# Layernorm, sliding attention and top-2 experts in one kernel: the first eight token tiles of QKV in a written order, two column groups in turn

## The chip, the cores and the metric

One core of a Trainium2 chip runs the whole program as one launch. The metric is the device time of that launch in microseconds (us); a time is the median of the runs shown. TensorE is called PE below, VectorE DVE, ScalarE ACT, GpSimd POOL; SyncE (SP) starts most of the DMAs.

## The reference

The input x is one sequence of 2048 tokens of 512 numbers, all in f32. The layernorm of x goes into two branches, and both are added to x:

```python
def attention(x, wqkv, wo):      # 32 heads of 16; 8 keys at distances 0, 2, .., 14
    q, k, v = split(x @ wqkv)
    idx = pos[:, None] - (arange(8) * 2)[None, :]
    logits = einsum("bhsd,bhswd->bhsw", q, k[idx]) * 16 ** -0.5   # -1e9 where idx < 0
    return einsum("bhsw,bhswd->bhsd", softmax(logits), v[idx]) @ wo

def experts(x, w_gate, w1, w2):  # 8 experts, 512 -> 1792 -> 512
    top2 = argsort(-(x @ w_gate))[:, :2]; gates = softmax(their logits)
    return sum over e of gate_e * (silu(x @ w1[e]) @ w2[e])

xn = layernorm(x)
out = x + attention(xn, wqkv, wo) + experts(xn, w_gate, w1, w2)
```

## The kernel before

**Numbers.** Every f32 factor of a matrix product is split into an f16 high and an f16 low part, and a product is three matmuls: high by high, high by low, low by high. The rows of `xh_j` hold both parts of token tile j after the layernorm; `xnT` holds the same turned (8 blocks of 128 × 128 per tile: four of the high, four of the low part). `wq_cg` holds the split columns of `wqkv` that belong to column group cg: 384 high columns (q, k and v of four chunks of two heads), for group 0 also 16 columns of the gate, and 384 low ones. `split_wq` makes them from the loaded `wqs_cg`, the high part on ACT, the low on DVE.

**Tiles.** The tokens lie in 16 tiles j of 128. `norm_tile(j)` takes `x_{j // 2}` (each load brings two tiles) and does: the moments on DVE (L226, L228), the root on ACT (L230), reciprocal and normalisation on DVE (L231, L233), the high part on ACT and the low part on DVE for tiles 0 and 1 and on POOL for the others (L235, L236). Tiles 0 to 5 are turned by PE (L241), eight blocks into a PSUM tile `pt_j`, and copied in one piece by ACT (odd tiles) or DVE (even ones). Tiles 6 to 15 are turned by one DMA each on SP (L248). `store_xn(j)` writes `xh_j` to `xr` in DRAM, for the experts' gathers.

**Products.** `qkv_tile(cg, j)` does twelve matmuls for one tile and one column group (L262 to L264), two evictions on ACT into `qe` and `ke` (L270, L272; two buffers each, of four tiles), for group 0 the 16 gate logits on DVE (L276), and after every fourth tile two stores on SP, of `qe` to `qd` and of `ke` to `kvd` (L281, L282). PSUM has six banks in turn for it.

**Order.** Group 0 comes first for all 16 tiles, then groups 1, 2 and 3. In this part of the program the tile framework's scheduler sets the order on each engine, from the order of the code and its own reckoning of when operands are ready. Routing follows group 0's last gate logits; POOL gathers the experts' token rows from `xr`, and SP turns them; the first of these turns is put behind the store of group 2's last four tiles (`FIRST`). From group 2 on, each tile is followed by pieces of the attention on DVE: `attend(QATT)` takes pieces from a list (`atoms`) as long as the sum of their costs is behind the sum granted. The experts follow, in an order written by hand, in steps of one hidden block: ACT makes the high part of the hidden values `hh` (L723, L724), DVE the low (L730) and the low part of the weights (L148), and in each step `EATT` (one number for large experts, one for small) is granted to the attention that is left. The pieces there are, among others, a product over 2048 columns (L567, L593) and the sums that fold it (L600).

**Start.** `warm_up(n, tag)` runs n products of zeros on PE, 12 at the start and 8 behind `norm_tile(1)`'s code. The loads on SP are: x_0 in two halves, the four parts of `wqs_0` (192 KB each), the gate's columns, then x_1 and on.

Of the kernel before, what the change touches and what calls it, by code (L numbers as in the profile page):

```python
# [9 lines left out]
F16 = mybir.dt.float16  # L10
# [47 lines left out]
def layer_kernel(ctx: ExitStack, tc, x, wqkv, wo, wg, w1, w2, out):  # L58
# [23 lines left out]
    root = cp.tile([P, 1], F32, name="root")  # L82
    nc.scalar.activation(root, eps, AF.Sqrt)
# [129 lines left out]
    load_x(0)
    load_wq(0)
    for g in range(1, 4):
        load_x(g)

    xhs = {}
# [3 lines left out]

    def norm_tile(j):
        xt = xg4[j // 2][:, j % 2, :]
        st = fre.tile([P, 6], F32, name=f"bs_{j}", tag="bs")
        nc.vector.bn_stats(st, xt)  # L226
        mv = fre.tile([P, 2], F32, name=f"mv_{j}", tag="mv")
        nc.vector.bn_aggr(mv, st)  # L228
        rs = fre.tile([P, 1], F32, name=f"rs_{j}", tag="rs")
        nc.scalar.activation(rs, mv[:, 1:2], AF.Sqrt, bias=eps, scale=1.0 / (SX * SX))  # L230
        nc.vector.reciprocal(rs, rs)  # L231
        xn = fre.tile([P, D], F32, name=f"xn_{j}", tag="xn")
        nc.vector.tensor_scalar(xn, xt, mv[:, 0:1], rs, op0=ALU.subtract, op1=ALU.mult)  # L233
        xh = fre.tile([P, 2, D], F16, name=f"xh_{j}", tag="xh", bufs=8)
        nc.scalar.copy(xh[:, 0, :], xn)  # L235
        (nc.vector if j < NDV else nc.gpsimd).tensor_tensor(xh[:, 1, :], xn, xh[:, 0, :], op=ALU.subtract)  # L236
        xhs[j] = xh
        if j < NPE:
            pt = py.tile([P, 2 * KB, P], F16, name=f"pt_{j}", tag="misc" if j % 2 else "yt")
            for a in range(2 * KB):  # L240
                nc.tensor.transpose(pt[:, a, :], xh[:, a // KB, (a % KB) * P:(a % KB + 1) * P], ident)  # L241
            dst = xnT[:, :, j * P:(j + 1) * P]
            if j % 2 == NEV:
                nc.scalar.copy(dst, pt)
            else:
                nc.vector.tensor_copy(dst, pt)  # L246
            return
        nc.sync.dma_start_transpose(out=xnT[:, :, j * P:(j + 1) * P], in_=xh.rearrange("p a d -> p (a d)"))  # L248

    tags = [(pu, "up"), (pu, "up"), (py, "y0"), (py, "y1"), (py, "y2"), (py, "y3")]  # L250
    ev, stored = {}, {}
    last = {"pe": None, "act": None, "dve": None, "dve0": None, "up": None}

    def qkv_tile(cg, j):
        pp, tg = tags[j % len(tags)]
        ps = pp.tile([P, 512], F32, name=f"pq_{cg}_{j}", tag=tg)
        t = wq[cg]
        n = 400 if cg == 0 else 384
        for kb in range(KB):
            xh = xnT[:, kb, j * P:(j + 1) * P]  # L260
            xl = xnT[:, KB + kb, j * P:(j + 1) * P]
            nc.tensor.matmul(ps[:, 0:n], xh, t[:, kb, 0:n], start=kb == 0, stop=False)  # L262
            nc.tensor.matmul(ps[:, 0:384], xh, t[:, kb, 400:784], start=False, stop=False)  # L263
            nc.tensor.matmul(ps[:, 0:n], xl, t[:, kb, 0:n], start=False, stop=kb == KB - 1)  # L264
# [5 lines left out]
        nc.scalar.activation(qe[:, :, j % 4, :], ps[:, 0:128].rearrange("p (c d) -> p c d", d=H2),  # L270
                             AF.Copy, scale=1.0 / (SW * SX))
        last["act"] = nc.scalar.activation(ke[:, :, j % 4, :, :].rearrange("p c a d -> p a c d"),  # L272
                             ps[:, 128:384].rearrange("p (a c d) -> p a c d", a=2, d=H2),
                             AF.Copy, scale=1.0 / (SW * SX))
        if cg == 0:
            nc.vector.tensor_scalar(glog[:, j, :], ps[:, 384:400], 1.0 / (SW * SX), None, op0=ALU.mult)  # L276
        if j % 4 == 3:
            qv = qd.rearrange("c (p j) d -> p c (j d)", j=NJ)
            kv = kvd[:, 16:, :].rearrange("c (p j) d -> p c (j d)", j=NJ)
            cs = slice(4 * cg, 4 * cg + 4)  # L280
            nc.sync.dma_start(qv[:, cs, g * 4 * H2:(g + 1) * 4 * H2], qe.rearrange("p c j d -> p c (j d)"))  # L281
            stored[cg, g] = nc.sync.dma_start(kv[:, cs, g * 8 * H2:(g + 1) * 8 * H2],  # L282
                                              ke.rearrange("p c j a d -> p c (j a d)"))

    for j in range(NJ):
        if j % 2 == 0 and j // 2 + 4 < NJ // 2:
            load_x(j // 2 + 4)
        norm_tile(j)
        if j == 0:
            split_wq(0)  # L290
        if j == 1:
            warm_up(8, "y1")
        if j == 8:
            load_wq(1)
        if j == 13:
            split_wq(1)
        if j == 6:
            fills()
        if j >= 5:
            store_xn(j - 5)  # L300
        if j > 1:
            qkv_tile(0, j - 2)
    qkv_tile(0, NJ - 2)
    qkv_tile(0, NJ - 1)
    for j in range(NJ - 5, NJ):
        store_xn(j)
# [742 lines left out]
```

## Time and profile before

| | |
|---|---|
| median of 3 runs | 797.95 us (797.6 to 799.4) |
| the profiled execution | 798.24 us, of it 796.4 from first to last instruction |
| PE, DVE, ACT, POOL busy | 779.9, 642.4, 379.0, 105.5 us |
| granted PE clock, mean | 0.997 |
| QKV's first product | 12.96 us after the span's start |
| QKV's last product ends, experts begin | 147.35 us |

A row of the profile names a group of instructions by line, engine, operation and tiles (output <- inputs), or one of them with its start and length. "Idle before" is the time for which the engine stood still just ahead of it, and the arrow names what ended that. L12 is line 12 of the kernel before, unless the text says otherwise.

### The profile page before, as it was taken

The page shows a single profiled execution, that of the slowest core. Times are in us where ns is not written, and L with a number is a line of the kernel's source. Part 1 is how long each engine was busy: PE and PEld are TensorE (multiplying, and loading weights), DVE is VectorE, ACT ScalarE, POOL GpSimd, SP SyncE. Part 2 cuts the span into 40 slices and gives each one's busy share as a digit, 9 for nine tenths or more (in the row PEclk, how much of TensorE's full clock was granted, in tenths as well). Part 3 has the DMA queues.
Part 4 walks back from the last instruction along what each step waited for, and adds up shares of the span by engine and source line. Part 5 has one row for each costly group of instructions (what it writes and reads, how often), then busy time and mean ns, then how long its engine had stood idle before and what let it go on. Part 6 is the DMA issues. An engine that isn't in the chain of part 4 may idle for free.

```text
span 796.4 us, 13794 instructions
## 1 busy us (share of the span) xinstructions
PE 779.9 (98%) x5318; PEld 427.2 (54%) x5318; DVE 642.4 (81%) x915; ACT 379.0 (48%) x706; POOL 105.5 (13%) x118
## 2 busy tenths in 40 slices
PE   7899999999999999999999999999999999999996
PEld 3556666555555555555555555555555555555543
DVE  7929998389888889799789879887999898736363
ACT  4644423564647364736364545545554645544100
POOL 3510502002000300030012000100100000023450
PEclk9999999999999999999999999999999999999999
DMA  8999949558347925573489446744955552594583
GB/s 288 253 295 317 330 159 246 156 144 238 110 142 191 290 81 169 169 232 111 135 220 257 150 136 185 219 156 128 272 174 169 158 155 85 160 329 165 157 281 117
DMA packets 152389, 153.89 MB, mean 193 GB/s; under 512 B 68000, under 2 KB 119456, under 8 KB 151808
## 3 DMA queue, kind: packets, MB, share of 16 engines
q1 hardware_dynamic: 147104, 136.09, 58.4%
q0 software_dynamic: 5216, 16.88, 7.2%
q8 instruction: 43, 0.70, 0.4%
q14 instruction: 26, 0.21, 0.1%
HBM read 108.12 MB, written 29.52 MB: 173 GB/s over the span
## 4 chain that ended last, share of the span: by engine, by line
PE 91%; DVE 3%; DMA 1%; ACT 1%; issue 1%; SPq 0%; POOL 0%; DVEq 0%; POOLq 0%; ACTq 0%
PE pu L718 12%; PE pu L720 12%; PE pu L719 12%; PE y L761 9%; PE y L763 9%; PE y L762 9%; PE pq L262 4%; PE pq L264 4%; PE pq L263 4%; PE yt L743 3%; PE yt L745 3%; PE yt L744 3%; PE pw L955 2%; PE pw L957 2%; PE pw L958 2%
## 5 line engine op out<-in xcount | busy, mean ns | idle before, releaser
L723 ACT ACTIVATE pu<-pu 128x512 f32<-128x512 f32 (+4 forms) x154 | 72.7, 472 | 249.2 <-PE pu L720 249.0
L718 PE MATMUL pu<-xgt,w 128*128 128x512 f16 (+4 forms) x616 | 185.0, 322 | 1.2 <-DVE hh L730 1.0
L719 PE MATMUL pu<-xgt,w 128*128 128x512 f16 (+4 forms) x616 | 185.3, 322 | 0.0
L720 PE MATMUL pu<-xgt,w 128*128 128x512 f16 (+4 forms) x616 | 181.0, 322 | 0.0
L148 DVE SCALAR_TENSOR_TENSOR w<-s,w 128x1024 f16<-128x1024 f32 x112 | 136.2, 1218 | 3.7 <-ACT w L143 3.5
L730 DVE SCALAR_TENSOR_TENSOR hh<-pu,hh 128x512 f16<-128x512 f32 (+4 forms) x154 | 80.3, 544 | 68.7 <-ACT hh L724 68.4
L763 PE MATMUL y<-w,hh 128*128 128x512 f16 x336 | 127.3, 379 | 0.0
L762 PE MATMUL y<-w,hh 128*128 128x512 f16 x336 | 127.3, 379 | 0.0
L761 PE MATMUL y<-w,hh 128*128 128x512 f16 x336 | 127.2, 379 | 0.0
L143 ACT ACTIVATE w<-s 128x1024 f16<-128x1024 f32 x112 | 116.9, 1048 | 2.8 <-DMA s<-in_B_w 2.8
L687 POOL DMA_INDIRECT xg<-xr,lis x35 | 51.6, 1473 | 482.2 <-DMA xgt<-xg 434.6
L262 PE MATMUL pq<-wq,xnT 128*128 128x384 f16 (+1 forms) x256 | 84.6, 330 | 5.0 <-DVE xnT L246 4.4
L720 PEld LDWEIGHTS <-w 128*128 128x128 f16 x616 | 57.3, 97 | 51.4
L264 PE MATMUL pq<-wq,xnT 128*128 128x384 f16 (+1 forms) x256 | 84.4, 330 | 0.0
L263 PE MATMUL pq<-wq,xnT 128*128 128x384 f16 x256 | 84.0, 328 | 0.0
L745 PE MATMUL yt<-hh,w 128*128 128x160 f16 (+4 forms) x448 | 83.6, 222 | 0.0
L743 PE MATMUL yt<-hh,w 128*128 128x160 f16 (+4 forms) x448 | 83.5, 222 | 0.0
L744 PE MATMUL yt<-hh,w 128*128 128x160 f16 (+4 forms) x448 | 83.5, 222 | 0.0
L719 PEld LDWEIGHTS <-w 128*128 128x128 f16 x616 | 57.3, 97 | 46.1 <-issue 2.0
L718 PEld LDWEIGHTS <-w 128*128 128x128 f16 x616 | 58.1, 97 | 44.4
L724 ACT ACTIVATE hh<-pu 128x512 f16<-128x512 f32 (+4 forms) x154 | 74.6, 484 | 4.9
L593 DVE TENSOR_TENSOR pv<-kvt,at 128x2048 f32<-128x2048 f32 x32 | 72.7, 2285 | 0.4
(189 smaller groups left out, 1033.5 us busy)
## 6 DMA issues: line engine op xcount, KB each, us to landing
s<-in_B_w SPq DMA_DIRECT2D x112, 512.0 KB, 3.9
kvt<-kvd SPq DMA_DIRECT2D x16, 960.0 KB, 5.3
kvd<-ke SPq DMA_DIRECT2D x16, 512.0 KB, 4.0
yd<-ys SPq DMA_DIRECT2D x24, 256.0 KB, 2.2
xr<-xh SPq DMA_DIRECT2D x16, 256.0 KB, 4.4
qd<-qe SPq DMA_DIRECT2D x16, 256.0 KB, 3.8
qt<-qd SPq DMA_DIRECT2D x16, 256.0 KB, 4.4
acc<-in_A_x SPq DMA_DIRECT2D x4, 1024.0 KB, 14.1
```

The lines of the kernel that those rows point to most:

```text
L143: nc.scalar.activation(w[:, :, 0, :], st, AF.Copy, scale=SW)
L148: nc.vector.scalar_tensor_tensor(w[:, :, 1, :], st, SW, w[:, :, 0, :], op0=ALU.mult, op1=ALU.subtract)
L262: nc.tensor.matmul(ps[:, 0:n], xh, t[:, kb, 0:n], start=kb == 0, stop=False)
L263: nc.tensor.matmul(ps[:, 0:384], xh, t[:, kb, 400:784], start=False, stop=False)
L264: nc.tensor.matmul(ps[:, 0:n], xl, t[:, kb, 0:n], start=False, stop=kb == KB - 1)
L718: last["pe"] = nc.tensor.matmul(ps, a_[:, kb, 0, fs], xh, start=kb == 0, stop=False)
L719: nc.tensor.matmul(ps, a_[:, kb, 0, fs], xl, start=False, stop=False)
L720: nc.tensor.matmul(ps, a_[:, kb, 1, fs], xh, start=False, stop=kb == KB - 1)
L745: nc.tensor.matmul(dst, b_[:, 1, cs], hi, start=False, stop=sp, skip_group_check=True)
L761: nc.tensor.matmul(ym[t], hi, b_[:, 0, :], start=st, stop=False)
L762: nc.tensor.matmul(ym[t], hi, b_[:, 1, :], start=False, stop=False)
L763: nc.tensor.matmul(ym[t], lo, b_[:, 0, :], start=False, stop=sp)
```

## The change

The first eight tiles (`NFIRST = 8`) are written by hand inside a block in which the order of the code is the order on PE, ACT, DVE, SP and POOL. In it both column groups 0 and 1 are computed for a tile before the next one; the later loop for group 1 starts at tile 8. `norm_tile` is cut into functions (`moments`, `deviation`, `normalize`, `x_high`, `x_low`, `turn_x`, `turned_x`, `turn_dma`), `qkv_tile` into `qkv_products`, `qkv_out` and `gate_out`. Further: `wqs_0` is loaded from ACT's queue, x_1 and `wqs_1` follow x_0 on SP; five tiles (`NPE`) instead of six are turned by PE, and each turned tile is copied in two halves, the high by ACT, the low by DVE; low parts are on POOL except for tile 0; the gate's columns are split on POOL; tile 0's products come by kind (high parts, low parts of x, low parts of weights, then eight products of 16 gate columns); `qe` and `ke` have their own tiles per column group out of the same two buffers; 15 warm-up products instead of 20; `QATT` and `EATT` have new values.

```diff
-QATT = 1.3
-EATT = (3.1, 2.78)
-NPE = 6
-NDV = 2
-NEV = 1
+QATT = 1.1
+EATT = (3.15, 2.86)
+NFIRST = 8
+NPE = 5
...
+    def qkv_product(cg, j, kb, pair, cols, first, end):
+        a, lo = pair
+        ps, t = pq[cg, j], wq[cg]
+        nc.tensor.matmul(ps[:, cols], xnT[:, a * KB + kb, j * P:(j + 1) * P],
+                         t[:, kb, 400:784] if lo else t[:, kb, cols], start=first, stop=end, skip_group_check=True)
...
+    def turned_x(j, a, copy):
+        copy(xnT[:, a * KB:(a + 1) * KB, j * P:(j + 1) * P], pts[j][:, a * KB:(a + 1) * KB, :])
...
+    load_x(0)
+    load_wq(0, (0, 1), nc.scalar)
+    nc.scalar.activation(root, eps, AF.Sqrt)
+    load_wq(0, (2, 3), nc.scalar)
+    load_x(1)
+    nc.sync.dma_start(gs, wg.rearrange("(kb p) e -> p kb e", p=P))
+    load_wq(1)
+    load_x(2)
+    load_x(3)
+    warm_up(WARM, "y0")
+    moments(0)
+    deviation(0)
+    wq_high(0, 0)
+    moments(1)
+    deviation(1)
+    normalize(0)
+    x_high(0)
...
+    for j in range(2, NFIRST):
+        qkv_products(0, j)
+        if j < 6:
+            load_x(j + 2)
+        if j + 2 < NFIRST:
+            moments(j + 2)
+            deviation(j + 2)
+        qkv_out(1, j - 1)
+        if j + 1 < NPE:
+            turn_x(j + 1, 0)
+            turn_x(j + 1, 1)
+            turned_x(j + 1, 0, act)
+            turned_x(j + 1, 1, dve)
+        if j + 2 < NFIRST:
+            normalize(j + 2)
+            x_high(j + 2)
+            x_low(j + 2, gp)
+            if j + 2 >= NPE:
+                turn_dma(j + 2)
+        qkv_products(1, j)
+        qkv_out(0, j)
+        gate_out(j)
+        store_xn(j - 2)
+    qkv_out(1, NFIRST - 1)
...
-        for j in range(NJ):
+        for j in range(NFIRST if cg == 1 else 0, NJ):
             qkv_tile(cg, j)
             if (cg, j) >= (2, 0):
                 attend(QATT)
```

The order on SP around the first tiles that the DMA turns. Rows are instructions in the order of the queue, with their line in the kernel that they belong to; `qd` and `kvd` are the stores (column group and group of four tiles in the second name), `xr` the row stores. Before, from tile 5's row store on:

```order
L221 DMA xr_68<-xh_5_374 128x1024
L248 DMA_TRANSPOSE xnT_144<-xh_6_417 128x8x128
L281 DMA qd_66<-qe_0_0_282 128x4x128
L282 DMA kvd_67<-ke_0_0_283 128x4x256
L221 DMA xr_68<-xh_6_417 128x1024
L248 DMA_TRANSPOSE xnT_144<-xh_7_451 128x8x128
```

After:

```order
L250 DMA_TRANSPOSE xnT_142<-xh_5_459 128x8x128
L298 DMA qd_66<-qe_0_0_292 128x4x128
L299 DMA kvd_67<-ke_0_0_293 128x4x256
L214 DMA xr_68<-xh_1_219 128x1024
L169 DMA x_6_495<-in_A_x 128x1024
L298 DMA qd_66<-qe_1_0_361 128x4x128
L299 DMA kvd_67<-ke_1_0_362 128x4x256
L250 DMA_TRANSPOSE xnT_142<-xh_6_510 128x8x128
```

Between the first two transposes stood three transfers, and six stand there now, with the stores of two column groups and an x load among them.

The order on DVE in the same place. Before, tiles 2 to 5 go in pairs, with the moments ahead (from the low part of tile 1 on):

```order
L226 BN_STATS bs_2_247<-x_1_173 128x6
L226 BN_STATS bs_3_287<-x_1_173 128x6
L228 BN_AGGR mv_2_249<-bs_2_247 128x2
L246 COPY xnT_144<-pt_0_193 128x8x128
L228 BN_AGGR mv_3_289<-bs_3_287 128x2
L226 BN_STATS bs_4_327<-x_2_175 128x6
L226 BN_STATS bs_5_365<-x_2_175 128x6
L231 RECIPROCAL rs_2_251<-rs_2_251 128x1
L231 RECIPROCAL rs_3_291<-rs_3_291 128x1
L233 TENSOR_SCALAR xn_2_254<-x_1_173,mv_2_249,rs_2_251 128x512
```

After, one tile at a time; the piece around tile 5, with the half copy of tile 4 (`pt_4`):

```order
L218 BN_STATS bs_5_437<-x_2_171 128x6
L220 BN_AGGR mv_5_439<-bs_5_437 128x2
L247 COPY xnT_142<-pt_4_445 128x4x128
L228 RECIPROCAL rs_5_441<-rs_5_441 128x1
L230 TENSOR_SCALAR xn_5_457<-x_2_171,mv_5_439,rs_5_441 128x512
L303 TENSOR_SCALAR glog_143<-pq_0_3_422 128x16
L218 BN_STATS bs_6_497<-x_3_173 128x6
```

Tile 0's turned copy stood behind the moments of tiles 2 and 3; now a tile's normalisation stands behind the half copy of the tile ahead of it.

The order on DVE where the experts begin: low parts of the first hidden blocks (`hh_0_0`, `hh_0_1`), of the weights (`w2_0_0`), and a piece of the attention (`pv`). Before:

```order
L730 SCALAR_TENSOR_TENSOR hh_0_0_2005<-pu_0_0_0_2006,hh_0_0_2005 128x512
L730 SCALAR_TENSOR_TENSOR hh_0_0_2005<-pu_0_0_512_2019,hh_0_0_2005 128x48
L600 TENSOR_TENSOR pv_1_0_1863<-pv_1_0_1863 128x8x64
L148 SCALAR_TENSOR_TENSOR w2_0_0_2040<-s2_0_0_1991,w2_0_0_2040 128x2x512
L730 SCALAR_TENSOR_TENSOR hh_0_1_2044<-pu_0_1_0_2045,hh_0_1_2044 128x512
```

After:

```order
L856 SCALAR_TENSOR_TENSOR hh_0_0_1999<-pu_0_0_0_2000,hh_0_0_1999 128x512
L856 SCALAR_TENSOR_TENSOR hh_0_0_1999<-pu_0_0_512_2013,hh_0_0_1999 128x48
L719 TENSOR_TENSOR pv_1_0_2036<-kvt_1_1379,at_1_1537 128x2048
L145 SCALAR_TENSOR_TENSOR w2_0_0_2034<-s2_0_0_1986,w2_0_0_2034 128x2x512
L856 SCALAR_TENSOR_TENSOR hh_0_1_2039<-pu_0_1_0_2040,hh_0_1_2039 128x512
```

The piece between the two hidden blocks was a fold over 512 columns and is now a product over 2048; the attention as a whole has moved back.

More of the change, by code (lines that the diff above doesn't have):

```diff
@@ L213, in layer_kernel, with load_wq @@
[L213 to L218, printed above, removed]
+    wv = wqkv.rearrange("(kb p) (t c) -> p kb t c", p=P, t=3)
+    def load_wq(cg, kbs=range(KB), queue=nc.sync):
+        if cg not in wqs:
+            wqs[cg] = (fre if cg < 2 else frp).tile([P, KB, 3, P], F32, name=f"wqs_{cg}",
+                                                    tag="wqs", bufs=2 if cg < 2 else 1)
+            wq[cg] = frp.tile([P, KB, 784], F16, name=f"wq_{cg}", tag="wq")
+        for kb in kbs:
+            queue.dma_start(wqs[cg][:, kb], wv[:, kb, :, cg * P:(cg + 1) * P])
@@ L220, in store_xn, with split_gate @@
+    def split_gate():
+        t = wq[0]
+        nc.gpsimd.tensor_scalar(gs, gs, SW, None, op0=ALU.mult)
+        nc.gpsimd.tensor_copy(t[:, :, 384:392], gs)
+        nc.gpsimd.tensor_tensor(t[:, :, 392:400], gs, t[:, :, 384:392], op=ALU.subtract)
+    xhs, mvs, rss, xns, pts = {}, {}, {}, {}, {}
     def store_xn(j):
         nc.sync.dma_start(xrv[:, j, :], xhs[j].rearrange("p a d -> p (a d)"))
-    def norm_tile(j):
[L224 to L248, printed above, removed]
@@ new lines, in x_high, with x_low, turn_x @@
+    def x_high(j):
+        xhs[j] = fre.tile([P, 2, D], F16, name=f"xh_{j}", tag="xh", bufs=8)
+        nc.scalar.copy(xhs[j][:, 0, :], xns[j])
+    def x_low(j, engine):
+        engine.tensor_tensor(xhs[j][:, 1, :], xns[j], xhs[j][:, 0, :], op=ALU.subtract)
+    def turn_x(j, a):
+        if a == 0:
+            pts[j] = py.tile([P, 2 * KB, P], F16, name=f"pt_{j}", tag="misc" if j % 2 else "yt")
+        for kb in range(KB):
+            nc.tensor.transpose(pts[j][:, a * KB + kb, :], xhs[j][:, a, kb * P:(kb + 1) * P], ident)
@@ new lines, in layer_kernel @@
+    start_cm.__enter__()
+    act, dve, gp = nc.scalar.copy, nc.vector.tensor_copy, nc.gpsimd
+    root = cp.tile([P, 1], F32, name="root")
+    load_x(0)
[13 more added lines that the diff above has]
+    deviation(1)
@@ new lines, in layer_kernel @@
+    normalize(0)
+    x_high(0)
+    normalize(1)
+    wq_high(0, 1)
+    turn_x(0, 0)
+    warm_up(2, "y1")
+    x_low(0, nc.vector)
+    x_high(1)
+    x_low(1, gp)
+    turn_x(0, 1)
+    warm_up(1, "y2")
+    turned_x(0, 0, act)
+    wq_low(0, 0)
+    turned_x(0, 1, dve)
+    for kb in range(1, KB):
+        if kb > 1:
+            wq_high(0, kb)
+        wq_low(0, kb)
+    qkv_bank(0, 0)
+    part = slice(0, 384)
+    for kb in range(KB):
+        qkv_product(0, 0, kb, (0, 0), part, kb == 0, False)
@@ new lines, in layer_kernel @@
+    for kb in range(KB):
+        qkv_product(0, 0, kb, (1, 0), part, False, False)
+    turn_x(1, 0)
+    turn_x(1, 1)
+    turned_x(1, 0, act)
+    turned_x(1, 1, dve)
+    split_gate()
+    for kb in range(KB):
+        qkv_product(0, 0, kb, (0, 1), part, False, kb == KB - 1)
+    for kb in range(KB):
+        for a in range(2):
+            qkv_product(0, 0, kb, (a, 0), slice(384, 400), False, kb == KB - 1 and a == 1)
+    qkv_products(0, 1)
+    wq_high(1, 0)
+    moments(2)
+    deviation(2)
@@ L304, in layer_kernel @@
     qkv_tile(0, NJ - 1)
-    for j in range(NJ - 5, NJ):
+    for j in range(NJ - 2, NJ):
         store_xn(j)
```

141 lines of the change are left out of this document (85 added, 56 removed).

## The prediction

> **What bounds the kernel now.** I read the page's first part and its chain, then a table of stretches, then that chain in order of time, and only then the groups of the early stretch. The page: TensorE is busy nearly all the time.
>
> ```profile
> span 796.4 us, 13794 instructions
> PE 779.9 (98%) x5318; PEld 427.2 (54%) x5318; DVE 642.4 (81%) x915; ACT 379.0 (48%) x706; POOL 105.5 (13%) x118
> PE 91%; DVE 3%; DMA 1%; ACT 1%; issue 1%; SPq 0%; POOL 0%; DVEq 0%; POOLq 0%; ACTq 0%
> ```
>
> So a change of order can win only where PE idles or runs slowly. The table shows where (start:end, length, then busy time of PE, its weight loads, DVE, ACT, POOL; granted clock, DMA share, GB/s):
>
> ```profile
> 5.70:9.20 3.50, 2.83 (x15) 1.16 (x13) 2.87 (x9) 3.33 (x8) 0.00 (x0) 1.00 0.96 251
> 9.20:12.70 3.50, 1.19 (x12) 0.68 (x12) 3.33 (x8) 1.36 (x3) 0.00 (x0) 1.00 1.01 375
> 12.96:16.10 3.14, 3.13 (x10) 1.49 (x11) 3.14 (x11) 0.91 (x2) 0.56 (x1) 0.50 1.03 364
> 16.10:30.00 13.90, 10.70 (x85) 6.86 (x83) 12.70 (x32) 10.38 (x27) 7.20 (x7) 1.00 0.94 278
> 30.00:46.88 16.88, 16.21 (x97) 9.12 (x95) 10.18 (x30) 9.52 (x30) 8.64 (x8) 1.00 1.16 239
> 46.88:147.35 100.47, 100.47 (x646) 60.67 (x647) 80.66 (x220) 36.26 (x117) 14.75 (x10) 1.00 0.86 269
> 160.00:780.00 620.00, 619.41 (x4296) 334.28 (x4294) 514.12 (x575) 306.31 (x501) 69.36 (x57) 1.00 0.62 180
> ```
>
> ```profile
> 12.96 0.52 PE L262 MATMUL pq<-wq,xnT 128*128 128x400 f16 x1 [1.82 <-DVE xnT L246]
> ```
>
> QKV's first product starts at 12.96. Between there and 46.88 PE loses 1.57 (3.14 us at half clock) + 3.20 (13.90 − 10.70) + 0.67 = 5.4 us. From 46.88 to the end of QKV (147.35), and in the experts, it loses nothing. So the most the change can gain is these 5.4 us and an earlier first product.
>
> **The start.** Rows of the chain (start, length) and of the timeline:
>
> ```profile
> 5.08 5.86 DMA x<-in_A_x
> 3.74 1.35 DVE L226 BATCH_NORM_STATS2 bs<-x 128x6 f32<-128x512 f32 x2 [1.56 <-DMA x<-in_A_x]
> 10.15 0.40 PE L241 MATMUL pt<-ident,xh 128*128 128x128 f16 x4 [0.45 <-DVE xh L236]
> 21.64 0.55 DVE L233 TENSOR_SCALAR xn<-x,mv,rs 128x512 f32<-128x512 f32 x1
> ```
>
> And the groups up to 54 us (busy, mean ns):
>
> ```profile
> L236 POOL TENSOR_TENSOR xh<-xn,xh 128x512 f16<-128x512 f32 x14 | 16.4, 1182 | 20.7 <-ACT xh L235 20.7
> L226 DVE BATCH_NORM_STATS2 bs<-x 128x6 f32<-128x512 f32 x16 | 10.7, 685 | 1.8 <-DMA x<-in_A_x 1.7
> L235 ACT CAST xh<-xn 128x512 f16<-128x512 f32 x16 | 9.7, 614 | 6.9 <-DVE xn L233 6.0 <-ACT rs L230 0.5 <-ACT ke L272 0.4
> L272 ACT ACTIVATE ke<-pq 128x256 f32<-128x256 f32 x16 | 6.0, 377 | 0.0
> L270 ACT ACTIVATE qe<-pq 128x128 f32<-128x128 f32 x16 | 4.4, 272 | 11.0 <-PE pq L264 9.5 <-issue 1.5
> L244 ACT COPY xnT<-pt 128x1024 f16<-128x1024 f16 x3 | 3.0, 1003 | 1.9 <-PE pt L241 1.9
> L228 DVE BATCH_NORM_AGGREGATE mv<-bs 128x2 f32<-128x6 f32 x16 | 2.7, 174 | 0.0
> L231 DVE RECIPROCAL rs<-rs 128x1 f32<-128x1 f32 x16 | 2.2, 147 | 0.6 <-ACT rs L230 0.5
> L246 DVE COPY xnT<-pt 128x1024 f16<-128x1024 f16 x3 | 2.0, 667 | 0.0
> L236 DVE TENSOR_TENSOR xh<-xn,xh 128x512 f16<-128x512 f32 x2 | 1.3, 686 | 0.0
> ```
>
> Today the chain goes through an x load that lands at 10.94 (5.08 + 5.86): DVE takes the moments of tiles 2 and 3 before it copies tile 0's turned block. The written order puts these behind tile 0, and the gate's split on POOL. DVE runs the moments of tile 1 before tile 0's reciprocal, so tile 0 waits for x_0's second half. That half is used at 3.74 + 0.69 = 4.4 today. The first 384 KB of weights now leave from ScalarE's queue at the same moment; at the 334 GB/s of the row below they cost that half up to 1.15 us. From 5.6: 0.69 + 0.17 (moments), 0.15, 0.55, 0.61 (high), 0.69 (low), 0.40 (turn), and a half copy on ACT of 0.58 (1.003 less four times the 0.105 by which a 128-column eviction is dearer), with some 0.06 of handing over at each of eight steps: 9.9. Gain 3.1 us; 2.3 if the weights' high and low parts come late, 4.2 if the weights cost x_0 nothing. The Trainium skill, page "DMA: Bandwidth & Descriptors", section "Issuing engines are not separate DMA queues", speaks against the other queue: transfers that different engines start share the same 16 DMA engines and interleave, and only the sequencer's issue time is saved. By it the gain is the 3.1, and without such sharing it would be the 4.2; no trace of before shows weights on ScalarE's queue.
>
> **The clock at the start.** In 9.20:12.70 PE was busy 1.19 of 3.50 and the clock was halved just behind it; in 5.70:9.20 it was busy 2.83 and stayed at full. In the changed order PE has between its twelve warm-up products (ending at about 6) and 9.9 only eight turns (0.8) and three warm-up products (about 1.0): in 5.7:9.2 some 1.6 of 3.5 us, nearer to the 1.19 than to the 2.83. I take the half clock for 9.2 to 12.7. It costs 2.8 / 2 = 1.4, less about 0.3 of waits for low weights that it covers: 1.1 (0 if the clock stays).
>
> **Column groups in turn.** PE's work is the same, +0.5 for eight products of the gate's 16 columns (at 0.06, about the 0.10 per turn of the row above less its handing over). In return each tile feeds 3.95 us of PE, not 2.0 (rows below), so the work on a tile 1 to 4 (DVE 0.69 + 0.17 + 0.15 + 0.55 + 0.39 = 2.0, ACT 0.61 + 0.58 + two evictions of 0.65 = 2.5) is covered: all of the 5.4 us goes. I keep 1.0 for small waits inside tiles 0 to 2 (weights' highs, a low part on POOL that now takes 1.18 where DVE took 0.69). If that cover were gone it would be the 3.20 again.
>
> **Tiles 5 to 7.** Tile 5 is now turned by the DMA, not by PE. The rows for it (landing of the transposes, PE's pace between two stores that are four tiles apart, rate, sizes):
>
> ```profile
> DMA to landing us min/median/max: 3.4/4.0/5.7
> 101.06 0.36 SPq L281 DMA_DIRECT2D qd<-qe  x1
> 108.86 0.36 SPq L281 DMA_DIRECT2D qd<-qe  x1
> 41.15 5.68 DMA xnT<-xh
> DMA packets 4492, 5.01 MB, mean 334 GB/s; under 512 B 1029, under 2 KB 3466, under 8 KB 4492
> x<-in_A_x SPq DMA_DIRECT2D x7, 512.0 KB, 7.8
> xr<-xh SPq DMA_DIRECT2D x11, 256.0 KB, 4.1
> kvd<-ke SPq DMA_DIRECT2D x3, 512.0 KB, 3.8
> qd<-qe SPq DMA_DIRECT2D x3, 256.0 KB, 3.9
> ```
>
> A tile of groups 1 to 3 takes PE 7.80 / 4 = 1.95, one of group 0 with eight of its twelve products 400 instead of 384 columns wide 2.00.
>
> - *Tile 5.* Its normalisation stands on DVE behind tile 4's turned half, and that behind the half on ACT. From PE's turn of tile 4: ACT's previous eviction 0.25, halves 0.58 + 0.39, reciprocal 0.15, normalise 0.55, high 0.61, low on POOL 1.18, transpose 4.0, handing over 0.35: 8.1 us. Meanwhile PE has three products: 1.95 + 2.00 + 1.95 = 5.9. Stall 2.2 (1.6 with the landing at 3.4, 3.9 at 5.7).
> - *Tile 6.* On SP's queue its transpose stands behind six transfers of 256, 512, 256, 512, 256 and 512 KB (the stores of both groups' tiles 0 to 3, a row store, an x load): 2304 KB, 7.1 us at 334 GB/s, against 3.95 us of cover in tile 5's two products. The nearest row is the one at 41.15: behind a 256 and a 512 KB store a transpose took 5.68, 2.3 above the least of 3.4, which is 768 KB at 334. Stall 7.1 + 0.5 − 3.95 = 3.7 (1.0 if the stores have half drained while SP waited for tile 5; 4.3 if the transposes too take engine time).
> - *Tile 7.* ACT cannot evict group 0's tile 4 until a store of group 0 has landed (two buffers), and tile 7's high part stands behind that eviction: 0.61 + 1.18 + 4.0 after it. Stall 1.2 (0 to 1.4). A tile behind (12): 0.5.
>
> Together 7.6. The transposes themselves are free if they land in time; they do not. Row stores, x loads and the second group's weights (4 × 192 KB early on SP) cost PE nothing else.
>
> **The experts' first steps.** Rows: attention steps on DVE, PE's wait for DVE and the wait of routing's gathers:
>
> ```profile
> L593 DVE TENSOR_TENSOR pv<-kvt,at 128x2048 f32<-128x2048 f32 x32 | 72.7, 2285 | 0.4
> 153.45 0.68 DVE L600 TENSOR_TENSOR pv<-pv 128x512 f32<-128x512 f32 x1
> PE pu L718 <- DVE hh L730: 1.0, 2, 0.6
> POOL xg L687 <- DMA qd<-qe: 43.6, 1, 43.6
> ```
>
> With 1.1 in place of 1.3 per QKV tile, 32 × 0.2 = 6.4 us of attention move into the experts. There DVE is at 514 of 620, and the two new rates (3.15, 2.86) spread them, 0.05 and 0.08 more a step, under the 17% that is idle: nothing. But behind the first hidden block DVE now has a 2.29 step where it had 0.68, and the second block's w2 and hidden values stand behind it: 1.6 later. PE waits there already (the 0.6), so little hides it, though two banks are in turn: +0.8, the middle of 0 and 1.6. The gate's logits come some eight products of group 1 (15.6 us) later, which routing can take: its gathers stood still for 43.6 us behind a store.
>
> **Sum** against the profiled execution: −3.1 (start) − 5.4 (losses of before) + 1.1 (clock) + 0.5 + 1.0 + 7.6 + 0.8 = +2.5. The profiled execution took 798.24, 0.29 over the median of the runs shown (797.95): 800.7, or 800.45 from the median. I say 800.5.
>
> **Rivals.**
> - *Transposes in time (faster).* The place is tile 5's transpose against the end of tile 4's second product, and from there SP's queue. For it: DVE and ACT are idle for 40% of 30:46.88, so the chain could start earlier than I have it. Against: the row at 41.15, and the order, which ties tile 5 to PE's turn of tile 4. With no stalls: 2.5 − 7.6 = −5.1, 793; with a third of them: 795.5. It decides where tile 5's landing is under 5.9 after the turn, and 2304 KB drain in 4 us, 576 GB/s against the 375 that is the most in these rows.
> - *Only tile 5 and half of tile 6.* SP issues the stores early, so half of the bytes have gone when tile 6 is ready: stalls 4.4 rather than 7.6: 797.3, no change. For it: the stores wait for nothing late and can drain while tile 6 is made. Against: all stand behind tile 5's transpose on SP, which issues in order.
> - *The clock halves in the gaps too.* PE idles 3.7 us before tile 6, more than the 2.3 of the 3.50 that brought the half clock at 12.96. Then 3.4 us at half, 1.7 lost, part of it in tile 7's wait: +1 to +1.7, 802. The Trainium skill, page "TensorE: Matmul & The Clock Gate", section "🎯 Why this matters for your kernels", warns of PE gaps above some 3 us between bursts, and puts the window of the gate at about 3.4 us; the trace agrees at 12.96:16.10 (3.14 us at 0.50).
> - *The change does not bring its data earlier*: x_0 comes at 5.6 or later and the start gains 2.3; +0.8, inside my range.
>
> **Chances.** As forecast, 799.3 (the clock stays) to 802: 0.45. Clock in the gaps, 802 to 804: 0.15. Half of the stalls (797.3): 0.20. Transposes in time (793 to 796): 0.20. The range, 795.0 to 803.5, leaves out half of the last case and the top of the second. A measurement can tell 0.2% (1.6 us) from no change: faster is below 796.35, slower above 799.55. From the cases: faster 0.22, within 0.18, slower 0.60. The likeliest case's own range is 799.3 to 802.
>
> **What the changed profile would show.** First product near 9.9, clock 0.50 in part of 9 to 13; PE without gaps from tile 1 to tile 4's second product; then waits of PE on the DMA of xnT at tile 5 (2), 6 (3.7) and 7 (1); QKV's end at 148 to 150 rather than 147.35; a wait of PE on hidden values at the second or third block. If the waits on xnT sum to under 4 us I am wrong on SP's queue; if PE shows no half clock, on the start; if QKV ends on time and the end does not, on the experts.

## The result, and the profile after

The changed kernel takes 808.1 us (807.06 to 810.61, 4 runs) against 797.98 (797.6 to 799.4, 4 runs): the ratio is 1.013, 95% interval 1.0112 to 1.0148. It is slower, as forecast, but by 10 us where 2.5 were forecast, and outside the range. Lines and times below are of the profiled execution of 807.98.

The page after, its span, its row of engines and its chain by engine:

```profile
span 806.3 us, 13773 instructions
PE 782.1 (97%) x5313; PEld 427.3 (53%) x5313; DVE 641.5 (80%) x914; ACT 378.4 (47%) x708; POOL 113.5 (14%) x122
PE 80%; DVE 10%; DMA 4%; ACT 2%; issue 2%; SPq 1%; POOL 1%; ACTq 0%; DVEq 0%; POOLq 0%
```

PE does nearly the same work in 10 us more, and DVE has gone from 3% to 10% of the chain. The table of stretches of the same execution (columns as before the change):

```profile
5.70:9.20 3.50, 1.71 (x13) 0.62 (x11) 2.87 (x8) 1.51 (x4) 0.00 (x0) 1.00 1.11 301
9.20:12.70 3.50, 2.44 (x19) 1.53 (x20) 2.10 (x4) 1.99 (x5) 2.48 (x4) 1.00 0.94 247
16.10:30.00 13.90, 13.24 (x96) 8.24 (x95) 7.04 (x20) 7.12 (x21) 3.53 (x3) 1.00 0.42 137
30.00:46.88 16.88, 11.18 (x60) 5.86 (x57) 9.08 (x27) 6.74 (x23) 4.61 (x4) 0.90 0.93 242
46.88:65.36 18.48, 16.03 (x96) 9.19 (x95) 8.46 (x23) 8.27 (x27) 8.03 (x7) 1.00 1.10 264
65.36:69.00 3.64, 3.64 (x15) 1.86 (x16) 0.04 (x1) 0.55 (x2) 0.00 (x0) 0.68 1.13 284
100.00:107.00 7.00, 6.05 (x40) 3.46 (x39) 7.00 (x38) 3.50 (x10) 0.00 (x0) 1.00 1.00 344
154.80:167.50 12.70, 9.95 (x79) 4.83 (x78) 10.83 (x16) 8.85 (x19) 0.00 (x0) 1.00 0.22 70
```

Up to 30 us the change does what it says: PE, idle for 3.20 in 16.10:30.00 before, is idle for 0.66, and no clock is halved. Then it loses 5.7 us in 30.00:46.88, 2.45 to 65.36, 0.95 in a stretch of routing, 2.75 where the experts begin, and runs at a lower clock twice (0.90 in 30.00:46.88, 0.68 in 65.36:69.00). The waits of PE in the timeline, and the first product:

```profile
10.17 1.80 PE L267 MATMUL pq<-wq,xnT 128*128 128x384 f16 x8 [1.26 <-ACT xnT L247]
34.72 4.13 PE L267 MATMUL pq<-wq,xnT 128*128 128x400 f16 x24 [1.22 <-DMA xnT<-xh]
43.33 7.00 PE L267 MATMUL pq<-wq,xnT 128*128 128x400 f16 x33 [4.48 <-DMA xnT<-xh]
65.36 4.85 PE L267 MATMUL pq<-wq,xnT 128*128 128x400 f16 x18 [2.12 <-DMA xnT<-xh]
103.86 2.10 PE L532 MATMUL pl<-oh_c,oh_p 128*128 128x40 f16 x13 [0.95 <-issue]
162.28 0.18 PE L844 MATMUL pu<-xgt,w 128*128 128x48 f16 x1 [1.75 <-DVE hh L856]
```

The waits at 34.72 and 43.33 are tiles 5 and 6; 65.36 is tile 12 of group 0. The last eviction of QKV ends at 155.64; before the change it ended at 148.11 (147.73 + 0.38). So 7.5 of the 9.9 us of span are lost in QKV and 2.4 behind it. The chain in order of time shows what the waits at 43.33 and 65.36 are made of:

```profile
32.89 0.63 ACT xh L235
33.54 0.48 SPq L299
34.07 0.53 SPq L214
34.66 1.22 SPq L169
35.98 0.65 SPq L298
36.73 0.62 SPq L299
37.44 5.84 DMA xnT<-xh
...
54.70 3.52 DMA qd<-qe
58.62 0.64 SPq L299
59.31 0.77 SPq L214
60.17 5.14 DMA xnT<-xh
```

Tile 6's turn is issued only after SP has issued the stores, and lands 5.84 later; the median of this kernel's turns is 3.5. Tile 12's turn stands behind a `kvd` store (L299) that waited for an eviction, which waited for an earlier store of `qe` to land. Neither tile was made late: POOL's low part of tile 6 was ready at 34.74 and its turn was issued at 37.44, that of tile 12 was ready at 53.54 and its turn was issued at 60.17. For tile 5 it is the making: its turn is issued at 31.47, as soon as its low part is ready (31.44).

Where routing's products begin, DVE stands still for the first expert's weights, and the one-hot rows (`oh_c`, `oh_p`) that PE needs stand behind them. Two rows of DVE after, and one of PE before:

```profile
99.38 1.23 DVE L145 SCALAR_TENSOR_TENSOR w<-s,w 128x1024 f16<-128x1024 f32 x1 [4.06 <-ACT w L140]
103.51 2.36 DVE L529 TENSOR_SCALAR oh_p<-io,where 128x128 f16<-128x128 f16 x14
75.86 0.28 PE L406 MATMUL pl<-oh_c,oh_p 128*128 128x40 f16 x5
```

After the wait of 0.95 at 103.86, thirteen of these products take 2.10 us, one for each of DVE's rows (2.36 for 14); before, five took 0.28, and at that pace thirteen would take about 0.5. So routing costs PE some 2.6 us, 0.95 of it as idle time.

### The profile page after: what moved, and what is told of

The parts are those of the page before. It is cut to its first block, busy times and chain, and to the rows that moved or that the text cites. A ratio compares the mean times of both kernels' runs of the same rounds, so it can differ in the third digit from the quotient of the medians.

```text
span 806.3 us, 13773 instructions
## 1 busy us (share of the span) xinstructions
PE 782.1 (97%) x5313; PEld 427.3 (53%) x5313; DVE 641.5 (80%) x914; ACT 378.4 (47%) x708; POOL 113.5 (14%) x122
## 4 chain that ended last, share of the span: by engine, by line
PE 80%; DVE 10%; DMA 4%; ACT 2%; issue 2%; SPq 1%; POOL 1%; ACTq 0%; DVEq 0%; POOLq 0%
PE pu L844 12%; PE pu L846 12%; PE pu L845 12%; PE y L887 9%; PE y L889 9%; PE y L888 9%; PE pq L267 4%; PE yt L869 3%; PE yt L871 3%; PE yt L870 3%; PE pw L1081 2%; PE pw L1083 2%; PE pw L1084 2%; DVE pq L693 2%; DVE at L697 1%
## 5 line engine op out<-in xcount | busy, mean ns | idle before, releaser
L267 PE MATMUL pq<-wq,xnT 128*128 128x384 f16 (+2 forms) x776 | 131.7, 330 | 9.9 <-DMA xnT<-xh 7.8
L813 POOL DMA_INDIRECT xg<-xr,lis x35 | 56.3, 1609 | 472.7 <-DMA xgt<-xg 411.9
L267 PEld LDWEIGHTS <-xnT 128*128 128x128 f16 x776 | 74.5, 99 | 62.5 <-DMA xnT<-xh 9.0
L846 PEld LDWEIGHTS <-w 128*128 128x128 f16 x616 | 57.3, 97 | 51.3
L693 DVE TENSOR_TENSOR pq<-kvt,qt 128x2048 f32<-128x2048 f32 x32 | 73.0, 2282 | 2.0 <-DMA kvt<-kvd 2.0
```

Source lines behind the costliest of these rows:

```text
L267: nc.tensor.matmul(ps[:, cols], xnT[:, a * KB + kb, j * P:(j + 1) * P], t[:, kb, 400:784] if lo else t[:, kb, cols], start=first, stop=end ...
L846: nc.tensor.matmul(ps, a_[:, kb, 1, fs], xh, start=False, stop=kb == KB - 1)
```

## The experiments

Gaps of PE are read from each kernel's timeline. Each set of runs has the kernel before beside it; its median was 797.55, 799.17, 797.63 and 799.35 in the four sets, so versions of different sets are compared by their ratios to it. There is one profile of each version; what is read from it holds for that execution.

**All eight tiles turned by PE.**

```diff
-NPE = 5
+NPE = 8
```

> The changed kernel with all eight first tiles turned by PE (NPE 8 instead of 5). Theory one (tiles 5 to 7 come late because their DMA turns stand in SP's queue): the gaps before tiles 5 and 6 (1.2 and 4.5 us) and the half clock behind the second (about 1.4) go, PE pays 24 turns of 0.057 = 1.4: 808.1 - 7.1 + 1.4 = 802.4 us; the 2.1 us wait before tile 12 stays. Rival (DVE, busy all the time from 112 to 150, limits the way to the experts, whatever PE does before): PE comes earlier and waits later, under 3 us gained, 805 or more.

804.27 us, ratio 1.0079 (1.0062 to 1.0096): some two fifths of the loss, 3.8 of the 5.7 expected. The waits on DMA turns of tiles 5 to 7 are gone, so these turns were part of the loss. But PE waits 2.21 us ahead of 40.78 for ACT's copy of a turned tile, while ACT itself stands 1.35 and 0.87 us for stores to land, and 2.95 ahead of 59.11 for the DMA's turn of tile 11, which was issued behind the stores of tiles 4 to 7.

**The first stores behind tile 6's turn.**

```diff
+            if cg < 2 and g == 0:
+                held.append(put)     # the two stores
+            else:
+                put()
...
                 turn_dma(j + 2)
+            if j + 2 == 6:
+                for put in held:
+                    put()
```

> The changed kernel with the four stores of the first four tiles (qd, kvd of both column groups, 1536 KB) put behind tile 6's turn on SP; nothing else moved. Theory one (queue): tile 6's turn is issued some 3 us earlier and lands in 3.4 us instead of 5.8, the gap of 4.5 falls to about 0 to 1 and the half clock behind it goes, tile 7 waits up to 2 more: 803.5 to 805.5. Rival (the turn by DMA is itself slow, or tile 6 is made late by ACT and POOL): the gap stays above 3, 807 or more.

812.02 us, 1.0176 (1.0154 to 1.0199): slower than the changed kernel. The gap at tile 6 is gone, so the queue was its cause; but tile 7 waits 6.92. PE's row, and ACT's:

```profile
52.47 37.14 PE L267 MATMUL pq<-wq,xnT 128*128 128x400 f16 x207 [6.92 <-DMA xnT<-xh]
42.17 0.28 ACT L289 ACTIVATE qe<-pq 128x128 f32<-128x128 f32 x1 [5.97 <-DMA qd<-qe]
```

ACT stands still for 5.97 us until a store has landed, since both column groups share two buffers of `qe`; tile 7's high part stands behind that eviction.

**Own buffers for each column group.**

```diff
-            ev[cg] = (frp.tile([P, 4, 4, H2], F32, name=f"qe_{cg}_{g}", tag="qe"),
-                      frp.tile([P, 4, 4, 2, H2], F32, name=f"ke_{cg}_{g}", tag="ke"))
+            ep = fre if cg == 0 and j < NFIRST else frp
+            ev[cg] = (ep.tile([P, 4, 4, H2], F32, name=f"qe_{cg}_{g}", tag="qe"),
+                      ep.tile([P, 4, 4, 2, H2], F32, name=f"ke_{cg}_{g}", tag="ke"))
```

> The changed kernel with two buffers of qe and ke for each of the two column groups in the first eight tiles, instead of two for both. Theory (ACT's evictions of groups 0 and 1 wait for stores that stand in SP's queue, and the turn of tile 12 stands behind those stores): the wait before tile 12 (2.1) and the half clock behind it (1.7) go, the gap at tile 6 stays: 804 to 805.5. Rival (tile 12 is late because POOL and DVE make tiles 8 to 12 late): no change, 807 to 809.

803.49 us, 1.0073 (1.0056 to 1.009): 4.6 us better by this one edit. Tile 12 no longer waits, nor do routing's products; PE runs through from 46.56. In the rows below, the first two are of PE at tile 6 and of ACT at the start, then come two of DVE and two stretches:

```profile
46.56 40.42 PE L267 MATMUL pq<-wq,xnT 128*128 128x400 f16 x229 [5.15 <-DMA xnT<-xh]
9.82 0.52 ACT L192 ACTIVATE wq<-wqs 128x384 f16<-128x384 f32 x1 [2.12 <-DMA wqs<-in_A_wqkv]
95.07 1.09 DVE L531 TENSOR_SCALAR oh_c<-io,col,tokf 128x40 f16<-128x40 f16 x5
106.94 3.49 DVE L145 SCALAR_TENSOR_TENSOR w<-s,w 128x1024 f16<-128x1024 f32 x3
9.20:12.70 3.50, 1.31 (x5) 0.64 (x6) 1.33 (x3) 2.35 (x5) 1.73 (x2) 0.67 0.66 173
12.70:16.10 3.40, 3.40 (x18) 2.06 (x17) 1.22 (x4) 1.01 (x2) 0.75 (x2) 0.50 0.96 301
```

The two stretches are part of why it was not more: in this execution the first product came at 11.39 and the clock was halved behind the start, as in the kernel before and not as in the changed one, with the same order there. ACT stood 2.12 us for a part of the first weights, in the changed kernel 1.09.

The two rows of DVE say that the 4.6 us are not the buffers' alone. The gate's last logits come at 75.41 here, as late as in the changed kernel (76.18), and the first expert's weights are loaded as late (91.18 against 92.04). But the scheduler put DVE's one-hot rows ahead of these weights here, and behind them in the changed kernel. So the rows do not wait for the weights here.

**Both of these.** `NPE = 8` and own buffers.

> The changed kernel with own buffers of qe and ke for each column group in the first eight tiles, and with all eight turned by PE. Theory (the loss is made of two waits, DMA turns behind stores in SP's queue, and evictions that wait for stores): with 803.5 for own buffers alone, the gaps at tiles 5 and 6 (1.4 and 5.3) and the half clock behind them (2.4) go, PE pays 1.4 for turns: 795 to 797. Rival (DVE, busy through routing and attention, limits what PE gains): 800 or more.

804.24 us, 1.0072 (1.005 to 1.0093): no better than either alone, so the theory that two waits make the loss fell. The waits on tiles 5 to 7 are gone, and PE waits for tile 11 and in routing instead (two rows of PE, one of DVE, and two pieces of the chain):

```profile
56.23 24.49 PE L267 MATMUL pq<-wq,xnT 128*128 128x400 f16 x148 [2.96 <-DMA xnT<-xh]
96.83 2.10 PE L533 MATMUL pl<-oh_c,oh_p 128*128 128x40 f16 x13 [0.78 <-issue]
92.36 1.22 DVE L145 SCALAR_TENSOR_TENSOR w<-s,w 128x1024 f16<-128x1024 f32 x1 [3.89 <-ACT w L140]
46.60 1.16 POOL xh L238
51.18 5.01 DMA xnT<-xh
```

Tile 11's low part is ready at 47.76 (46.60 + 1.16), but its turn is issued at 51.18, behind the four stores of tiles 4 to 7 of both groups, and lands 5.01 later. With a turn issued at once and landing in 3.5, tile 11 would have been there at 51.3, ahead of the 53.27 at which PE began to wait. So the theory's own first cause, a DMA turn behind the stores of two groups, was not removed but came again at the next four tiles. And DVE waits 3.89 us for the first expert's weights (their load is issued at 85.24 us, before the change at 68.71, since it waits for routing), with routing's one-hot rows queued behind. The changed kernel has the same DVE wait, 4.06. In this execution the clock was also lower there (0.81 in 94.00:102.00).

**Own buffers, and the first stores behind tile 6's turn.** The diffs of "The first stores behind tile 6's turn" and "Own buffers for each column group" together, with five tiles turned by PE.

> Own buffers, and the four stores of the first four tiles behind tile 6's turn on SP; tiles 5 to 7 turned by the DMA. Theory (what delays tile 6 is the 1536 KB of stores ahead of its turn, and what delayed tile 7 when only the stores were moved was ACT waiting for these): gap at tile 6 about 1, at tile 7 about 1 to 2, no long half clock: 796.5 to 799. Rival (the turns by DMA come late of themselves): 802 or more.

806.68 us, 1.0113 (1.0084 to 1.0142). A miss: tile 6 does not wait, but tile 7's turn, issued at 42.19 behind the four stores, lands 5.42 later and PE waits 5.55; its low part was ready at 38.69 (37.53 + 1.16). The queue of 1536 KB moved from one tile to the next. Routing's products wait too, 1.62.

**The new attention rates alone**, in the kernel before.

```diff
-QATT = 1.3
-EATT = (3.1, 2.78)
+QATT = 1.1
+EATT = (3.15, 2.86)
```

> The kernel before with the new attention rates alone (1.1 per QKV tile; 3.15 and 2.86 per expert step). By the prediction's term: +0.8 (0 to 1.6), 798.8. If the 2.2 us at the experts' start of the changed kernel come from the rates alone: 800. If they come from the late gate logits: no change, 798.

799.38 against 799.17 us, 1.0006 (0.9995 to 1.0016): no change that can be told. From the start of QKV's last eviction to the end it is 649.6 us, before 648.7: +0.9 in one profile, as the prediction's term had it (+0.8). In the changed kernel it is 651.0. Beside PE's wait of 0.59 for hidden values there is now one of 1.00; the changed kernel has 1.75 and 1.00.

**The old attention rates in the changed kernel.** The reverse of this diff.

> The changed kernel with the attention's old rates (1.3 per QKV tile, 3.1 and 2.78 per expert step). Theory (the 2.2 us by which PE waits longer for hidden values at the experts' start come from the new rates alone): 806 or so, PE's wait on DVE hh back at about 0.6. Rival (they come from attention and routing that run late, since the gate's last logits come 15 to 25 us later): the wait stays or grows, 808 or more.

812.69 us, 1.0195 (1.0178 to 1.0212): a miss in sign, 4.6 slower. PE waits 5.70 for hidden values instead of 1.75 and 1.00; the chain ahead of it is DVE's work on attention and weights (156.40 to 164.30). So the new rates do not make the 2.2 us alone; in this kernel the old ones cost more.

**Column groups not in turn.** Group 0 alone in the first eight tiles:

```diff
-    qkv_products(1, 0)
...
-        qkv_out(1, j - 1)
-        qkv_products(1, j)
-        for j in range(NFIRST if cg == 1 else 0, NJ):
+        for j in range(NJ):
```

> The changed kernel without column groups in turn: in the first eight tiles only group 0, group 1 for all 16 tiles in the later loop. Everything else of the written order stays. Theory (the turns by DMA of tiles 5 to 7 stand behind stores whichever group is computed; in turn a tile covers 3.95 us, alone 2.0): the gap at tile 6 halves with half of the stores, but tiles 2 to 5 now wait 0.5 to 1 each: 801 to 806. Rival (computing two groups in turn is itself the loss, through twice the stores and shared buffers): 798 or less.

811.99 us, 1.0161 (1.0139 to 1.0183). Slower still, and outside both ranges. Ahead of the turns and products of tiles 2 to 4 PE waits 5.2 us in all (1.69, 0.90, 0.68, 0.68, 0.54, 0.68), in the changed kernel 0.65 (0.36 and 0.29). Behind them it waits for DMA turns (4.00, 2.13, 1.27, 0.61 and 2.06). So two groups in turn do cover the making of a tile.

**The clock behind tile 6's wait.** 16 products of zeros ahead of tile 6's:

```diff
     for j in range(2, NFIRST):
+        if j == 6:
+            warm_up(16, "yt")
```

> The changed kernel with 16 products of zeros on PE ahead of tile 6's products, where PE stands still for 4.5 us. Theory (the clock is halved because PE stands still there, and the half clock costs another 1.4 behind it): the wait for tile 6's turn stays, the clock stays at 1.00 from 43 to 47, 806.5. Rival (the half clock costs nothing, since tile 7 would wait in its place): 808.

808.69 us, 1.0148 (1.0124 to 1.0172), the same as without. The stretch behind the wait, in the changed kernel and here:

```profile
43.30:47.00 3.70, 3.67 (x14) 1.83 (x15) 2.23 (x7) 2.53 (x10) 2.39 (x3) 0.61 1.18 244
```

```profile
43.30:47.00 3.70, 2.17 (x13) 1.01 (x12) 1.39 (x4) 2.27 (x8) 1.16 (x1) 1.00 1.12 275
```

The clock stays at 1.00, so it is the standing still that halves it. But the total does not move: PE waits more for later tiles (in the second row it is busy for 2.17 of 3.70; it waits 0.52 for tile 7, for which the changed kernel does not wait, and 3.51 for tile 11). The profiled execution had a half clock at its start (some 2 us), the changed one's had not, so of the size no more can be said than that the two intervals leave no gain above about 1 us.

**The first weights back on SP's queue**, and, in the kernel before, on ScalarE's.

```diff
-    load_wq(0, (0, 1), nc.scalar)
+    load_wq(0)
     nc.scalar.activation(root, eps, AF.Sqrt)
-    load_wq(0, (2, 3), nc.scalar)
```

In the kernel before, the four loads of `wqs_0` are started by `nc.scalar` in place of `nc.sync`.

> The changed kernel with the first weights on SP's queue behind x_0, ahead of x_1. Theory (sharing): first product within 0.5 of 10.2 either way, the total within 1 us of 808. Rival (ScalarE's queue brings the early start): first product 1.5 or more later, 810.

> The kernel before with the four parts of the first weights on ScalarE's queue, nothing else. By the rule that the queues share the DMA engines: only issue time is saved, the x loads behind them on SP start 2.6 us earlier but share the engines, the first product comes 0 to 1.5 us earlier, and the total moves by less than that: 797.5 to 799. Rival (a queue of its own brings the data earlier): first product at 11 or before, 796.

On SP: 806.52 us, 1.0122 (1.0103 to 1.0142), against the changed kernel's 1.013 (1.0112 to 1.0148): the intervals overlap. On ScalarE's queue in the kernel before: 800.1, 1.0042 (1.0028 to 1.0056), slower. The first products, on SP and then in the kernel before with the other queue:

```profile
8.61 1.80 PE L267 MATMUL pq<-wq,xnT 128*128 128x384 f16 x8 [0.46 <-ACT xnT L247]
```

```profile
14.45 0.52 PE L262 MATMUL pq<-wq,xnT 128*128 128x400 f16 x1 [0.80 <-DVE xnT L246]
```

8.61 instead of 10.17, and 14.45 instead of 12.96: with the second queue the start came 1.5 us later in both pairs of profiles. All four expectations of the first product fell: both rivals, which had the second queue bring it earlier, and both theories, with half a microsecond in the changed kernel and a gain in the kernel before. The size varies: over all versions with the written order the first product comes at 8.61 to 8.99 with these weights on SP's queue (four versions), and at 9.48 to 11.51 with them on ScalarE's (ten).

**Four tiles in the written order instead of eight.** Own buffers (diff above), tiles 0 to 7 turned by PE, of which 4 to 7 in the scheduler's order; two x loads move behind the written order with them. Own buffers and eight tiles turned by PE were in the version of "Both of these" as well (1.0072), so what is new against it is the shorter written order.

```diff
-NFIRST = 8
-NPE = 5
+NFIRST = 4
+NPE = 4
...
         x_low(j, nc.gpsimd)
+        if j < 8:
+            for a in range(2):
+                turn_x(j, a)
+                turned_x(j, a, (nc.scalar.copy, nc.vector.tensor_copy)[a])
+            return
         turn_dma(j)
```

> A version with the written order and the two groups in turn for four tiles instead of eight, own buffers for each group, tiles 0 to 7 turned by PE (4 to 7 in the scheduler's order), tiles 8 to 15 by the DMA. Theory (the early start of 2.8 us is kept, the gate's logits come 8 us later instead of 16, and no turn stands behind the first stores): 794 to 798. Rival (any delay of the gate's logits delays the first expert weights and stalls routing, or tiles 8 to 15 come late): 800 or more.

797.5 against 797.63 us, 0.9994 (0.9982 to 1.0005), inside the theory's range: the loss is gone. Three more were run with the first weights on SP's queue: this one, the same with six tiles (`NFIRST = NPE = 6`), and this one with the old attention rates.

> The four-tile version (own buffers, tiles 0 to 7 turned by PE) with the first weights back on SP's queue. Theory (weights on ScalarE's queue delay x_0 by 1.5 us, as the changed kernel and the kernel before with that one edit showed): first product near 8.0 instead of 9.5, 796 against 797.5. Rival (a later wait takes the 1.5 us): no change, 797.5.

> The same with six tiles in the written order. Theory (the gate's logits four us later than with four tiles are still early enough, but tiles 8 to 15 are prepared later and wait): 797 to 800. Rival (routing stalls as with eight tiles, 3 us): 800 or more.

> The four-tile version on SP's queue with the attention's old rates (1.3; 3.1 and 2.78). Theory (with gate logits only 8 us later DVE can do the old share of attention in QKV; the rates alone cost nothing): the same time within 0.5. Rival (as in the eight-tile version, where the old rates cost 4.6 us: attention is not done when the experts begin): 799 or more.

Against 799.35 us in this set: four tiles 795.08, 0.9963 (0.9948 to 0.9978), faster than both kernels by a small margin: its five times (794.84 to 795.77) all lie under the lowest of the kernel before's 21 (797.06). The first product comes at 8.80, against 9.52 with ScalarE's queue, so only 0.7 of the expected 1.5 us; the profiled spans of the two are 793.6 and 793.7, so no trace shows where the rest of the gain comes from. For the others: six tiles 797.08, 0.9981 (0.9971 to 0.9992), inside the theory's range; four with the old rates 799.54, 1.0009 (0.9998 to 1.002). The four-tile version on SP's queue, its page and its stretches:

```profile
span 793.6 us, 13828 instructions
PE 779.1 (98%) x5337; PEld 427.4 (54%) x5337; DVE 641.9 (81%) x917; ACT 379.5 (48%) x711; POOL 111.8 (14%) x122
12.00:30.00 18.00, 16.24 (x114) 9.79 (x113) 16.94 (x47) 12.43 (x39) 8.10 (x7) 1.00 0.92 324
30.00:46.88 16.88, 15.14 (x104) 9.24 (x104) 10.61 (x31) 9.71 (x27) 8.09 (x7) 1.00 1.12 261
46.88:143.50 96.62, 96.62 (x623) 58.31 (x622) 74.07 (x218) 35.11 (x114) 15.46 (x10) 1.00 0.86 254
```

It loses 3.5 us from 12.00 to 46.88 and nothing from there to QKV's end, with no half clock. The gate's last logits come at 57.5 us here, 67.4 with six tiles, 69.3 with eight and own buffers, 76.2 in the changed kernel, 53.7 before. With six, as with own buffers alone (75.41), no wait of DVE for weights ahead of routing's rows shows, and DVE has the one-hot rows ahead of the weights. In each of the eight versions in which the weights stand ahead, DVE waits 2.50 to 5.57 us for them. So that wait comes from the order on DVE and not from the lateness alone. The old rates cost 4.5 us at four tiles too, by another chain than at eight: SP's last store of QKV stands there behind a weight load that waits for DVE, it lands at 153.8, and the first hidden values wait for it. So at four tiles that cost is one of order at the experts' start, and not of late logits; the expectation that it would be the same time fell.

## Why the prediction was right in sign and wrong in size

By its own terms, predicted and then measured in the profiled execution:

| term | predicted | measured |
|---|---|---|
| first product | −3.1 | −2.8 (10.17 against 12.96) |
| losses of before | −5.4 | gone |
| half clock at the start | +1.1 | 0 here; in other versions with this start there |
| products of the gate's columns | +0.5 | not measured alone |
| waits in tiles 0 to 2 | +1.0 | +0.75 |
| tiles 5, 6, 7 | +7.1 | +5.7 (1.22, 4.48, 0) |
| tile 12 and a small wait | +0.5 | +2.45 |
| half clock behind 43 and 65 us | 0 (a rival) | about +3.1 (1.4 and 1.7) |
| routing | 0 | about +2.6 |
| behind QKV | +0.8 | +2.4 |
| sum | +2.5 | +9.3 of the 9.9, with the 0.5 as predicted |

The sign is in part luck. Take the terms that the prediction priced, tile 12 and the steps behind QKV at its prices and the others as measured: they add up to about nothing (−2.8 − 5.4 + 0.5 + 0.75 + 5.7 + 0.5 + 0.8 = +0.05). What made the kernel slower are terms that it had at nothing or far too small. Three steps failed.

*Tile 12: "A tile behind (12): 0.5".* The prediction has the coupling (two buffers for two groups, so ACT waits for a store), but prices it for tile 7, at 1.2, and for tile 12 hardly at all. In the changed kernel ACT does wait just ahead of tile 7's high part, 1.60 and 1.10:

```profile
41.01 0.28 ACT L289 ACTIVATE qe<-pq 128x128 f32<-128x128 f32 x1 [1.60 <-DMA qd<-qe]
42.39 0.38 ACT L291 ACTIVATE ke<-pq 128x256 f32<-128x256 f32 x1 [1.10 <-DMA kvd<-ke]
```

But PE stands for tile 6 until 43.33 and then runs at half clock, and tile 7 is there in time. With the stores moved still later ACT waits 5.97, and tile 7 6.92. The same coupling holds for the next four tiles of each group: tile 12's turn stands behind a store that waits for an eviction that waits for a store, and PE waits 2.12, with a half clock behind it. Own buffers took this away, and 4.6 us in all, of which a part is routing's other order in that version.

*Routing: "The gate's logits come some eight products of group 1 (15.6 us) later, which routing can take: its gathers stood still for 43.6 us".* The logits come 22.5 us later (76.18 against 53.69). The reason given looks at the gathers alone. The loads of the first expert's weights wait for routing too: they came 23 us later (92.04 against 68.71), DVE stood 4.06 us for them with the one-hot rows behind, and routing cost PE some 2.6. The lateness does this only together with the order on DVE: with own buffers the logits are as late and routing costs PE no wait. It is also argued, not shown, that attention pieces that are late for this reason make the rest of the 2.4 us behind QKV, of which the rates alone make some 0.9.

*The clock in the gaps*, a rival with a chance of 0.15, was left out of the sum. "The clock halves in the gaps too" came true (0.61 in 43.30:47.00 behind tile 6, 0.65 in 65.36:70.21 behind tile 12, which is 1.4 and 1.7 us lost); its 802 was short because the other terms were not in it. The Trainium skill, page "TensorE: Matmul & The Clock Gate", section "🎯 Why this matters for your kernels", warns of gaps above some 3 us. The trace agrees behind tile 6's 4.48, and differs behind the wait of 2.12 at 65.36, where the clock fell too; in the version with eight tiles turned by PE it held behind one of 2.21. What the half clocks cost in the end stays open: the run with zeros shows that without the first of them other waits come up.

The start was sized well. The second half of x_0 is used at 5.32, where the prediction had 5.6; with the weights on SP's queue it is used at 4.27, so sharing costs it 1.05, near the worst case of 1.15. What the working left to its case of 2.3 is that the weights come late as well: ACT stands 1.09 us for the second part, with tile 0's copy behind it. Together the second queue costs 1.5 us. The Trainium skill's page "DMA: Bandwidth & Descriptors", section "Issuing engines are not separate DMA queues", says that the transfers interleave, and that a second issuing engine saves only the time to start them. The traces agree that the transfers share; they differ in that here it was a loss. The rival "does not bring its data earlier" fell with the 2.8.

The waits of tiles 5 and 6 were right in place and cause, and together in size (5.70 against 5.9): tile 5 waits for its making (1.22, predicted 2.2), tile 6's turn stands behind the stores (4.48, predicted 3.7). The rival "transposes in time" fell with the rows at 34.72 and 43.33, "only tile 5 and half of tile 6" with the 4.48. QKV's end, which the prediction had at 148 to 150, came at 154.89.

How the 10 us split stays open within these limits: the terms are read from one execution, and where one wait was removed another came up.

## What to carry to other kernels

Work on more outputs per input tile covers the making of the next tile, but it takes buffers, stores and queue places from the same pools at twice the pace: give each stream its own buffers before writing such an order, and look what stands ahead of each small urgent transfer in the queue (here also for tiles 11 and 12, behind the written order). Ask what the delayed outputs release (here the gate's logits: routing, then the loads of the first weights), and what stands behind a wait for that on each engine, not only whether their nearest reader has slack. Stop the written order as soon as its cover is no longer needed: eight tiles lost 1.3%, with own buffers and PE's turns 0.7%, and four of these lost nothing; with the first weights on SP's queue four gained 0.4%.

## What was not expected of the hardware

Starting the first weights from a second queue delayed the first product by 1.5 us in two kernels (10.17 against 8.61, 14.45 against 12.96 us) and by 0.7 in the four-tile version (9.52 against 8.80). The granted clock held at 1.00 in and behind a stretch with PE busy for 1.71 of 3.50 us, was halved after 1.19 of 3.50 in the kernel before, and fell in the version with own buffers within a stretch of 1.31 of 3.50 (0.67 in 9.20:12.70). It fell behind a wait of 2.12 us in one version and held behind one of 2.21 in another, so no threshold can be read from these runs.
